# The output product of a gated feed-forward by seven half-size products

## The chip, the cores and the metric

The program runs on one NeuronCore of a Trainium2 chip. TensorE (PE in the profile) multiplies, and its weight loads are listed apart (PEld). VectorE (DVE), ScalarE (ACT) and GpSimd (POOL) work element by element. SyncE (SP) only issues transfers here, and so do ACT and POOL beside their other work. Each engine takes its own instructions in order and waits for the others by semaphores. The metric is the device time of one execution in microseconds; of several executions the median is given.

## What is computed

For each of B = 4 batches, with N = 6016 rows and C = 256 columns, columns of q and k are normalised over the rows, s = knᵀ qn is a 256x256 matrix, a is its softmax, and x = v a. All 24064 rows of x then go through a gated feed-forward with 1536 hidden columns:

```python
s = kn.transpose(0, 2, 1) @ qn / tau          # 256x256 for each batch
a = exp(s - max) / sum
x = (v @ a).reshape(24064, 256)
gate = 1 / (1 + exp(-(x @ w_gate)))           # w_gate, w_val: 256x1536
val = x @ w_val
out = (gate * val) @ w_out                    # w_out: 1536x256
```

## The kernel before, in words

The matrix a is not applied to v. For each batch it is multiplied into the two weight matrices once (`gh_mms`, `gh_store`), which gives G = a w_gate and H = a w_val, so that gate and val come straight from v.

The 6016 rows of a batch are 47 tiles of 128 rows. They are worked through in 12 chunks (`ci` 0 to 11) of 4 tiles, the last of 3: 48 chunks in all. A chunk has 12 steps, here called slots (`f` 0 to 11), one for each 128 hidden columns. A slot does this (`glu`, L414):

- PE forms ps_gate (2 matmuls of 512 columns, one PSUM bank) and ps_val (2 more) from the transposed v;
- ACT writes g_sb, the sigmoid of ps_gate (L435);
- DVE multiplies ps_val by g_sb into hT (L436), which is hidden-by-row, so that it can be the stationary operand of the product that follows;
- PE does 4 matmuls of 256 columns of the output product of the chunk *before* this one (`out_mms`, L442): hT is loaded as weights, w_out is streamed, and 12 of them make one 128-row tile of the output in ps_o.

A finished ps_o is copied to out_sb by DVE in the slot after (`flush`, L458, copy at L462), and when a chunk's last tile is copied, SP stores it. All pools for ps_gate, ps_val and ps_o have two buffers, so the gate matmuls of slot f+2 need the sigmoid of slot f, and the val matmuls of slot f+2 need the product of slot f.

The order is written by hand (`manual_schedule`): what stands first in the program text comes first on each engine. Into the slots of batch b, `side_work` (L548) puts the preparation of batch b+1:

- chunks 0 to 7: loads of q and k (`load_qk`, issued on POOL, converted to bf16 on the way), the matmuls of s (`score`, 94 pairs of 256 columns), and for the norms the squares of q and k and their sums (`acc_square`, L209, and `acc_add`, L218, both on DVE);
- chunk 8: the sums are folded (`acc_fold`, six DVE steps);
- chunks 9 and 10 ("block" chunks): the output matmuls of the chunk before are not interleaved, but stand as one block of 48 after the 12 slots, and beside them run `wide_sqrt`, `wide_inv`, `wide_scale` and `exps`, whose functions need other tables on ACT than the sigmoid;
- chunk 11: G and H of the next batch.

Batch 3 has no side work. v is loaded by POOL two chunks ahead (`load_v`), and SP transposes it by DMA. At the start the whole q and k of batch 0 are loaded with `qkpool` of 8 buffers, then the weights; w_out comes in one POOL transfer in the first slot of the first chunk (`load_w_out`, L151). The end of the last chunk is written apart (`last_rows`, L466).

## Time and profile before

| | |
|---|---|
| median of 3 runs | 829.14 us (828.76 to 829.39) |
| profiled execution, first to last instruction | 827.4 us |
| mean granted TensorE clock | 0.996 |
| PE, DVE, ACT, POOL busy | 97%, 71%, 47%, 10% |
| matmuls of the output product | 2244 of 256 columns and 24 of 128 |
| a slot without side work | 1.30 us |
| a block chunk (198.54 to 214.14) | 15.60 us |

The profiled execution has no time beside its span; the median of the runs is 1.7 us above the span, and that 1.7 us is taken as what lies around it. Each line of the groups gives engine, operation, output and inputs, the shapes, how many, then busy time and mean duration, then the idle time of the engine just before. A line of the timeline begins with start and duration in us, and runs of the same instruction are merged ("x8"); matmuls overlap, so the spacing of a run is its length less one duration, divided by the number less one.

### The profile page before, as it was taken

What the parts mean: (1) busy time and instruction counts of PE and PEld (TensorE: products, weight loads), DVE (VectorE), ACT (ScalarE), POOL (GpSimd) and SP (SyncE); (2) the same over time, 40 slices, a digit from 0 to 9 for tenths busy, and PEclk for the clock granted to TensorE, in tenths of its full rate; (3) what the DMA queues carried; (4) which work ended last, traced back from release to release, by engine and by line L of the source; (5) the groups of instructions that cost most, each with busy time, mean ns of one, the idle gap of its engine ahead of it and who ended that gap; (6) DMA issues with size and microseconds to landing.
All of it is one profiled execution on the core that took longest, in us unless ns stands there. A gap on an engine that the chain in (4) does not pass through costs nothing.

```text
span 827.4 us, 13618 instructions
## 1 busy us (share of the span) xinstructions
PE 806.2 (97%) x5122; PEld 498.6 (60%) x5134; DVE 590.3 (71%) x1023; ACT 392.0 (47%) x643; POOL 79.0 (10%) x151
## 2 busy tenths in 40 slices
PE   3899999999999999999999999999999999999998
PEld 2556666665665666665575666666566566666666
DVE  5777877787667777778757777777766666666665
ACT  3754444446644444445654444444655444444442
POOL 4432100002201100000221010000000000000000
PEclk9899999999999999999999999999999999999999
DMA  9999723327746443223976452223322323322211
GB/s 213 206 201 189 133 52 90 61 52 140 158 85 118 96 90 61 52 52 87 153 141 126 78 110 57 51 64 74 64 62 63 72 52 85 59 58 69 47 36 71
DMA packets 77874, 77.17 MB, mean 93 GB/s; under 512 B 50672, under 2 KB 55792, under 8 KB 77808
## 3 DMA queue, kind: packets, MB, share of 16 engines
q0 software_dynamic: 22768, 38.81, 28.2%
q1 hardware_dynamic: 54752, 36.91, 17.6%
q8 instruction: 40, 0.66, 0.3%
q10 hardware_dynamic: 288, 0.59, 0.2%
q14 instruction: 26, 0.21, 0.1%
HBM read 78.64 MB, written 24.64 MB: 125 GB/s over the span
## 4 chain that ended last, share of the span: by engine, by line
PE 94%; DMA 4%; DVE 1%; issue 0%; ACT 0%; POOL 0%; ACTq 0%; POOLq 0%
PE ps_o L88 30%; PE ps_val L88 29%; PE ps_gate L88 29%; PE ps_s L88 4%; DMA k_sb<-in_k_dram 3%; PE ps_gh L88 2%; DMA w_gate<-in_moe_w_gate_dram 1%; DVE hT L436 0%; ACT g_sb L435 0%; DVE sq L184 0%; PE ps_end L88 0%; PE ps_n L88 0%; DVE gh_G L385 0%; POOL q_sb L98 0%; PE ps_tp L403 0%
## 5 line engine op out<-in xcount | busy, mean ns | idle before, releaser
L436 DVE TENSOR_TENSOR hT<-ps_val,g_sb 128x512 bf16<-128x512 f32 (+1 forms) x576 | 391.2, 680 | 204.6 <-ACT g_sb L435 200.3
L435 ACT ACTIVATE g_sb<-ps_gate 128x512 bf16<-128x512 f32 (+1 forms) x576 | 338.2, 588 | 387.0 <-PE ps_gate L88 380.9
L88 PE MATMUL ps_gate<-vT,gh_G 128*128 128x512 bf16 (+1 forms) x1152 | 337.5, 375 | 0.2
L88 PE MATMUL ps_val<-vT,gh_H 128*128 128x512 bf16 (+1 forms) x1152 | 337.5, 375 | 0.3
L88 PE MATMUL ps_o<-w_out_sb,hT 128*128 128x256 bf16 x2244 | 324.9, 273 | 0.0
L88 PEld LDWEIGHTS <-hT 128*128 128x128 bf16 x2268 | 221.0, 98 | 124.6
L88 PEld LDWEIGHTS <-gh_H 128*128 128x128 bf16 x1152 | 112.7, 98 | 131.4 <-issue 1.0
L88 PEld LDWEIGHTS <-gh_G 128*128 128x128 bf16 x1152 | 112.3, 98 | 37.8 <-DVE gh_G L385 0.4
L462 DVE COPY out_sb<-ps_o 128x256 f32<-128x256 f32 x187 | 77.4, 414 | 12.6 <-PE ps_o L88 12.6
L88 PE MATMUL ps_s<-k_sb,q_sb 128*128 128x256 bf16 x376 | 70.1, 289 | 15.9 <-DMA k_sb<-in_k_dram 8.5
L108 POOL DMA_DIRECT2D v_sb<-in_v_dram x48 | 25.5, 532 | 609.5 <-DMA vT<-v_sb 473.8
L88 PEld LDWEIGHTS <-q_sb 128*128 128x128 bf16 x376 | 38.7, 103 | 24.2 <-issue 9.9
L223 DVE TENSOR_TENSOR acc<-acc,sq 128x1024 bf16<-128x1024 bf16 (+1 forms) x66 | 44.2, 670 | 0.0
L184 DVE TENSOR_TENSOR sq<-q_sb 128x1024 bf16<-128x1024 bf16 (+2 forms) x42 | 28.0, 667 | 1.1 <-DMA q_sb<-in_q_dram 1.1
L98 POOL DMA_DIRECT2D q_sb<-in_q_dram x44 | 24.3, 552 | 28.3 <-PE ps_s L88 10.7
L98 POOL DMA_DIRECT2D k_sb<-in_k_dram x44 | 24.0, 546 | 15.5 <-DMA k_sb<-in_k_dram 10.1
L184 DVE TENSOR_TENSOR sq<-k_sb 128x1024 bf16<-128x1024 bf16 (+2 forms) x34 | 22.4, 658 | 0.1
L182 ACT ACTIVATE sq<-k_sb 128x1024 bf16<-128x1024 bf16 (+1 forms) x11 | 10.7, 1010 | 11.9 <-DMA k_sb<-in_k_dram 11.9
L88 PE MATMUL ps_gh<-w_gate,e_sb 128*128 128x512 bf16 x41 | 12.7, 379 | 1.3 <-DMA w_gate<-in_moe_w_gate_dram 1.2
L88 PE MATMUL ps_gh<-w_val,e_sb 128*128 128x512 bf16 x45 | 13.5, 379 | 0.2
L88 PEld LDWEIGHTS <-e_sb 128*128 128x128 bf16 x112 | 10.2, 97 | 5.7 <-ACT e_sb L324 1.3
L435 ACT ACT_TABLE_LOAD x6 | 7.7, 1283 | 9.0 <-PE ps_gate L88 9.0
(68 smaller groups left out, 122.5 us busy)
## 6 DMA issues: line engine op xcount, KB each, us to landing
out_dram<-out_sb SPq DMA_DIRECT2D x44, 512.0 KB, 2.9
v_sb<-in_v_dram POOLq DMA_DIRECT2D x44, 256.0 KB, 3.9
q_sb<-in_q_dram POOLq DMA_DIRECT2D x35, 256.0 KB, 6.3
k_sb<-in_k_dram POOLq DMA_DIRECT2D x35, 256.0 KB, 7.1
q_sb<-in_q_dram POOLq DMA_DIRECT2D x4, 512.0 KB, 11.5
k_sb<-in_k_dram POOLq DMA_DIRECT2D x4, 512.0 KB, 13.4
out_dram<-out_sb SPq DMA_DIRECT2D x3, 384.0 KB, 3.5
w_gate<-in_moe_w_gate_dram POOLq DMA_DIRECT2D x3, 256.0 KB, 8.1
```

What stands on the lines that cost most here:

```text
L88: nc.tensor.matmul(out, lhsT=lhsT, rhs=rhs, start=start, stop=stop, **kw)
L98: nc.gpsimd.dma_start(out=tl[:, :nt, :], in_=rows(src, b)[:, t0 : t0 + nt, :])
L108: nc.gpsimd.dma_start(out=v_sb[:, :nt, :], in_=rows(v, b)[:, t0 : t0 + nt, :])
L182: nc.scalar.activation(out=sq[:, :nt, :], in_=src[:, :nt, :], func=ACT.Square)
L184: engine.tensor_tensor(out=sq[:, :nt, :], in0=src[:, :nt, :], in1=src[:, :nt, :], op=ALU.mult)
L223: nc.vector.tensor_tensor(out=acc[:, :nt, :], in0=acc[:, :nt, :], in1=st[b]["sq", w][:, :nt, :], op=ALU.add)
L435: nc.scalar.activation(out=g_sb[:, :n], in_=ps_gate[:, :n], func=ACT.Sigmoid)
L436: nc.vector.tensor_tensor(out=hts[b, ci][:, f, :n], in0=ps_val[:, :n], in1=g_sb[:, :n], op=ALU.mult)
L462: nc.vector.tensor_copy(out=out_sb[:, s, :], in_=ps)
```

## The change

The output product is done by Strassen's scheme. For a pair of 128-row tiles (tile p of the first half of the chunk and tile p of its second half), the hidden blocks (even and odd) and the two halves of the output columns, a 2x2 by 2x2 block product is formed with 7 products in place of 8. Each product is 6 matmuls of 128 columns, so a chunk of 4 tiles has 84 of these in place of 48 of 256. The chunks of 3 tiles do one pair so and the third tile as before; the last chunk of all is as before.

- Sums of hT blocks: 10 DVE instructions per chunk of 128x768 (`a_sum`), five (g = 0, hidden blocks 0 to 5) in slots 6 to 10 of the chunk itself, five (g = 1, blocks 6 to 11) in slots 0 to 4 of the next chunk, each behind the product into hT of that slot.
- Sums of w_out blocks: w_out is loaded as three fp32 pieces by SP into a pool of two buffers shared with the first q and k tiles; POOL converts it and forms the five sums (`sum_w_out`).
- Copies from PSUM: for each pair one of 512 and one of 384 columns, on ACT (`evict`), into m_sb.
- Recombination: five POOL instructions per pair (`combine`), then the store (in slot 4 of the chunk after the next).
- The squares of q and k for batches 1 to 3 go from DVE to ACT; g_sb is fp32.
- Buffers: qkpool 8 to 5, sqpool 3 to 2.

The diff, cut to its core:

```diff
+A_SUMS = (
+    ((0, 1), ALU.subtract, (1, 1)),
+    ((0, 0), ALU.add, (1, 1)),
+    ((0, 0), ALU.add, (0, 1)),
+    ((1, 0), ALU.add, (1, 1)),
+    ((1, 0), ALU.subtract, (0, 0)),
+)
+B_SUMS = (
+    ((1, 0), ALU.subtract, (0, 0)),
+    ((0, 1), ALU.subtract, (1, 1)),
+    ((1, 0), ALU.add, (1, 1)),
+    ((0, 0), ALU.add, (1, 1)),
+    ((0, 0), ALU.add, (0, 1)),
+)
+PRODUCTS = (
+    ((1, 1), 0),
+    ((0, 0), 1),
+    (0, 2),
+    (1, 3),
+    (2, (1, 1)),
+    (3, (0, 0)),
+    (4, 4),
+)
+FIRST_BANK = 4
...
-    qkpool = pool("qkpool", 8)
-    sqpool = pool("sqpool", 3)
+    f32pool = pool("f32pool", 2)
+    qkpool = pool("qkpool", 5)
+    sqpool = pool("sqpool", 2)
+    spool = pool("spool", 1)
+    mpool = pool("mpool", 2)
...
-    first_f32 = [consts.tile([P, nt, C], FP32, name=f"first{w}") for w in range(2)]
+    first_f32 = [f32pool.tile([P, TPC, C], FP32, tag="f32", name=f"first{w}") for w in range(2)]
...
-    def load_w_out():
-        nc.gpsimd.dma_start(out=w_out_sb, in_=moe_w_out.rearrange("(t p) c -> p t c", p=P))
+    w_sums = consts.tile([P, len(B_SUMS), FC // 2, P], BF16)
+    w_f32 = {}
+    def load_w_out(n):
+        w_f32[n] = f32pool.tile([P, TPC, C], FP32, tag="f32", name="w_f32")
+        nc.sync.dma_start(
+            out=w_f32[n], in_=moe_w_out.rearrange("(t p) c -> p t c", p=P)[:, n * TPC : (n + 1) * TPC, :]
+        )
+    def sum_w_out(n):
+        w = w_f32.pop(n)
+        nc.gpsimd.tensor_copy(out=w_out_sb[:, n * TPC : (n + 1) * TPC, :], in_=w)
+        for m, ((k0, c0), op, (k1, c1)) in enumerate(B_SUMS):
+            nc.gpsimd.tensor_tensor(
+                out=w_sums[:, m, n * 2 : (n + 1) * 2, :],
+                in0=w[:, k0::2, ds(c0 * P, P)],
+                in1=w[:, k1::2, ds(c1 * P, P)],
+                op=op,
+            )
...
-        if g == 0:
-            nc.vector.tensor_tensor(out=acc, in0=src, in1=src, op=ALU.mult)
-        else:
-            st[b]["sq", w] = squares(b, t0, nt, w, nc.vector)
+        st[b]["sq", w] = squares(b, t0, nt, w, nc.scalar, acc if g == 0 else None)
...
-        g_sb = gpool.tile([P, CH], BF16, tag="g", name="g_sb")
+        g_sb = gpool.tile([P, CH], FP32, tag="g", name="g_sb")
+    sums = {}
+    def a_sum(b, ci, g, m):
+        nt = groups[ci][1]
+        half = nt // 2
+        hT = hts[b, ci]
+        if m == 0:
+            sums[b, ci, g] = spool.tile(
+                [P, len(A_SUMS), FC // 4, CH // 2], BF16, tag=f"s{g}", name="sums", bufs=2 - g
+            )
+        (r0, k0), op, (r1, k1) = A_SUMS[m]
+        f0, f1 = g * (FC // 2), (g + 1) * (FC // 2)
+        nc.vector.tensor_tensor(
+            out=sums[b, ci, g][:, m, :, : half * P],
+            in0=hT[:, f0 + k0 : f1 : 2, ds(r0 * half * P, half * P)],
+            in1=hT[:, f0 + k1 : f1 : 2, ds(r1 * half * P, half * P)],
+            op=op,
+        )
-    def out_mms(b, ci, n0, n1):
-        t0, nt = groups[ci]
+    pending = []
+    stores = []
+    def out_tile(b, ci):
+        if (b, ci) not in ffn:
+            ffn[b, ci] = opool.tile([P, TPC, C], FP32, tag="osb", name="out_sb")
+        return ffn[b, ci]
+    def combine(b, ci, p, m):
+        half = groups[ci][1] // 2
+        blocks = out_tile(b, ci).rearrange("p t (h c) -> p (t h) c", c=P)
+        c00, c11 = 2 * p, 2 * (half + p) + 1
+        ends = blocks[:, c00 : c11 + 1 : c11 - c00, :]
+        t = m[:, 2:7:4, :]
+        nc.gpsimd.tensor_tensor(out=t, in0=t, in1=m[:, 3:4, :].to_broadcast([P, 2, P]), op=ALU.add)
+        nc.gpsimd.tensor_tensor(out=t, in0=t, in1=m[:, 4:6, :], op=ALU.subtract)
+        for n, mids in enumerate((c00 + 1, c11 - 1)):
+            nc.gpsimd.tensor_tensor(
+                out=blocks[:, mids, :], in0=m[:, 1 - n, :], in1=m[:, 4 + n, :], op=ALU.add
+            )
+        nc.gpsimd.tensor_tensor(out=ends, in0=t, in1=m[:, 0:2, :], op=ALU.add)
+    def out_work(b, ci):
+        nt = groups[ci][1]
+        half = nt // 2
-        for n in range(n0, min(n1, nt * FC)):
-            s, f = divmod(n, FC)
-            if n == 0:
-                ffn[b, ci] = opool.tile([P, TPC, C], FP32, tag="osb", name="out_sb")
+        work = []
+        def product(state, p, n, i):
+            a, w = PRODUCTS[n]
+            bank, first = (0, 0) if n < FIRST_BANK else (1, FIRST_BANK)
+            if n == first and i == 0:
+                state[bank] = pso.tile([P, CH], FP32, tag="o", name="ps_o")
+            g, j = divmod(i, FC // 4)
+            if isinstance(a, tuple):
+                lhsT = hT[:, 2 * i + a[1], ds((a[0] * half + p) * P, P)]
+            else:
+                lhsT = sums[b, ci, g][:, a, j, ds(p * P, P)]
+            rhs = w_out_sb[:, 2 * i + w[0], ds(w[1] * P, P)] if isinstance(w, tuple) else w_sums[:, w, i, :]
+            mm(
+                state[bank][:, ds((n - first) * P, P)],
+                lhsT,
+                rhs,
+                start=(n == first and i == 0),
+                stop=(i == FC // 2 - 1),
+                skip_group_check=True,
+            )
+            if i == FC // 2 - 1 and n in (FIRST_BANK - 1, len(PRODUCTS) - 1):
+                pending.append((evict, state, bank, p))
+        def evict(state, bank, p):
+            if bank == 0:
+                state["m"] = mpool.tile([P, len(PRODUCTS), P], FP32, tag="m", name="m_sb")
+            n0, n1 = (0, FIRST_BANK) if bank == 0 else (FIRST_BANK, len(PRODUCTS))
+            m = state["m"]
+            nc.scalar.copy(m[:, n0:n1, :], state[bank][:, : (n1 - n0) * P].rearrange("p (n c) -> p n c", c=P))
+            if bank == 1:
+                combine(b, ci, p, m)
+                if p == half - 1 and nt % 2 == 0:
+                    stores.append((b, ci))
+        def single(state, s, f):
-                ffn["ps"] = pso.tile([P, C], FP32, tag="o", name="ps_o")
-            mm(ffn["ps"], hT[:, f, ds(s * P, P)], w_out_sb[:, f, :], f == 0, f == FC - 1)
+                state["ps"] = pso.tile([P, CH], FP32, tag="o", name="ps_o")
+            mm(state["ps"][:, :C], hT[:, f, ds(s * P, P)], w_out_sb[:, f, :], f == 0, f == FC - 1)
-                pending.append((ffn[b, ci], s, ffn["ps"], b, ci))
-    pending = []
+                pending.append((evict_single, state, s))
+        def evict_single(state, s):
+            nc.scalar.copy(out_tile(b, ci)[:, s, :], state["ps"][:, :C])
+            stores.append((b, ci))
+        for p in range(half):
+            state = {}
+            for n in range(len(PRODUCTS)):
+                for i in range(FC // 2):
+                    work.append((1, product, state, p, n, i))
+        if nt % 2:
+            state = {}
+            for f in range(FC):
+                work.append((2, single, state, nt - 1, f))
+        return work
+    def run_work(work, share):
+        left = sum(w[0] for w in work)
+        upto = left * share
+        done = 0
+        while work and done < upto:
+            cost, fn, *args = work.pop(0)
+            fn(*args)
+            done += cost
-            out_sb, s, ps, b, ci = pending.pop(0)
+            fn, *args = pending.pop(0)
+            fn(*args)
+    def store():
+        while stores:
+            b, ci = stores.pop(0)
-            nc.vector.tensor_copy(out=out_sb[:, s, :], in_=ps)
-            if s == nt - 1:
-                nc.sync.dma_start(out=out_rows[b][:, t0 : t0 + nt, :], in_=out_sb[:, :nt, :])
+            nc.sync.dma_start(out=out_rows[b][:, t0 : t0 + nt, :], in_=ffn.pop((b, ci))[:, :nt, :])
+    def end_rows(b, ci, s):
+        hT = hts[b, ci]
+        ps = pso.tile([P, CH], FP32, tag="o", name="ps_o")
+        for f in range(FC):
+            mm(ps[:, :C], hT[:, f, ds(s * P, P)], w_out_sb[:, f, :], f == 0, f == FC - 1)
+        nc.vector.tensor_copy(out=out_tile(b, ci)[:, s, :], in_=ps[:, :C])
...
-                at(0, load_w_out)
+                for i in range(FC // TPC):
+                    at(i, load_w_out, i)
+                    at(i + 2, sum_w_out, i)
...
-                if prev is not None and not block:
-                    out_mms(*prev, f * TPC, (f + 1) * TPC)
+                if prev is not None:
+                    if f == 4:
+                        store()
+                    if not block:
+                        run_work(work, 1 / (FC - f))
+                    if f < len(A_SUMS):
+                        a_sum(*prev, 1, f)
+                if f >= FC // 2 and f - FC // 2 < len(A_SUMS) and (b, ci) != (B - 1, NCH - 1):
+                    a_sum(b, ci, 0, f - FC // 2)
...
-                    out_mms(*prev, s * FC, (s + 1) * FC)
+                    run_work(work, 1 / (TPC - s))
+            if prev != (B - 1, NCH - 1):
+                work = out_work(*prev)
+    flush()
-        out_mms(*prev, s * FC, (s + 1) * FC)
-        flush()
+        end_rows(*prev, s)
+    store()
```

## The prediction

> **What bounds the kernel now.** I read the page first, engines and then the chain.
>
> ```profile
> PE 806.2 (97%) x5122; PEld 498.6 (60%) x5134; DVE 590.3 (71%) x1023; ACT 392.0 (47%) x643; POOL 79.0 (10%) x151
> PE 94%; DMA 4%; DVE 1%; issue 0%; ACT 0%; POOL 0%; ACTq 0%; POOLq 0%
> ```
>
> PE is the bound from end to end; the 4% of DMA is the load of batch 0. So matmul time saved is time saved, as long as the other engines keep up. Next the groups, shapes kept apart, for the prices:
>
> ```profile
> L436 DVE TENSOR_TENSOR hT<-ps_val,g_sb 128x512 bf16<-128x512 f32 x528 | 364.4, 691 | 180.5 <-ACT g_sb L435 178.8 <-PE ps_gate L88 0.4
> L435 ACT ACTIVATE g_sb<-ps_gate 128x512 bf16<-128x512 f32 x528 | 315.1, 597 | 369.1 <-PE ps_gate L88 369.1
> L223 DVE TENSOR_TENSOR acc<-acc,sq 128x1024 bf16<-128x1024 bf16 x60 | 40.9, 682 | 0.0
> L184 DVE TENSOR_TENSOR sq<-q_sb 128x768 bf16<-128x768 bf16 x3 | 1.6, 550 | 0.0
> L237 DVE TENSOR_TENSOR two<-two 128x256 f32<-128x256 f32 x6 | 2.5, 415 | 0.0
> L182 ACT ACTIVATE sq<-k_sb 128x1024 bf16<-128x1024 bf16 x10 | 10.1, 1049 | 11.6 <-DMA k_sb<-in_k_dram 11.6
> masks.py:199 POOL TENSOR_SCALAR_AFFINE_SELECT ident_f<-ident_f 128x128 f32<-128x128 f32 x1 | 0.3, 292 | 0.1
> ```
>
> Then the timeline: one slot of batch 3, four DVE instructions back to back, the matmul spacings of 256 and 128 columns, and ACT and PE around the two block chunks.
>
> ```profile
> 701.73 0.59 PE L88 MATMUL ps_gate<-vT,gh_G 128*128 128x512 bf16 x2
> 702.36 0.60 ACT L435 ACTIVATE g_sb<-ps_gate 128x512 bf16<-128x512 f32 x1 [0.70 <-PE ps_gate L88]
> 702.59 0.60 PE L88 MATMUL ps_o<-w_out_sb,hT 128*128 128x256 bf16 x4
> 702.99 0.69 DVE L436 TENSOR_TENSOR hT<-ps_val,g_sb 128x512 bf16<-128x512 f32 x1 [0.61 <-ACT g_sb L435]
> ...
> 58.18 0.69 DVE L436 TENSOR_TENSOR hT<-ps_val,g_sb 128x512 bf16<-128x512 f32 x1 [0.83 <-ACT g_sb L435]
> 58.79 0.41 DVE L462 COPY out_sb<-ps_o 128x256 f32<-128x256 f32 x1
> 59.12 0.68 DVE L214 TENSOR_TENSOR acc<-q_sb 128x1024 bf16<-128x1024 bf16 x1
> 59.72 0.69 DVE L436 TENSOR_TENSOR hT<-ps_val,g_sb 128x512 bf16<-128x512 f32 x1
> ...
> 822.69 1.51 PE L88 MATMUL ps_end<-w_out_sb,hT 128*128 128x128 bf16 x24
> 198.54 5.40 PE L88 MATMUL ps_o<-w_out_sb,hT 128*128 128x256 bf16 x48
> ...
> 200.63 1.28 ACT L435 ACT_TABLE_LOAD   x1
> 216.05 0.91 ACT L332 ACTIVATE e_sb<-x_sb,shift 128x256 bf16<-128x256 f32 x2 [0.24 <-DVE x_sb L274]
> ```
>
> From a slot's first gate matmul, the sigmoid starts at 0.63, the output matmuls at 0.86, the product into hT at 1.26 us. DVE instructions overlap: 0.61 from the product to the next, 0.60 from a 0.68 add. Matmul spacing: (5.40-0.27)/47 = 0.109 for 256 columns, (1.51-0.22)/23 = 0.056 for 128, each with new weights.
>
> **A. Matmuls, -23.9 us.** 2220 of 256 columns (242.2 us) become 44 x 84 + 3 x 42 = 3822 of 128 (214.4) and 36 of 256 (3.9). A slot shrinks from 1.30 to 0.86 + 7 x 0.056 = 1.26. The nearest row for narrow matmuls is the burst of 24 at the end; between wide ones they may be slower, bounded by the 256-column spacing of 0.109 (third rival), or no better than 0.056. I take 0.056.
>
> The Trainium skill, "TensorE: Matmul & The Clock Gate", section "Back-to-back issue gap", speaks against the change: for a stream of weight load and matmul pairs it gives about 81 ns at 128 columns. By that A would be 3822 x 0.081 + 3.9 - 242.2 = +71 us; the burst's 0.056 decides here.
>
> **Engines beside PE.** An a_sum is 768 elements from two SBUF inputs: 0.55 by the row of squares, 0.47 to the next instruction. DVE loses 187 copies and, in batches 1 to 3, the squares, and gains 10 sums a chunk: 12 x 0.61 + 10 x 0.47 = 12.0 of 15.1 us. With 3 adds (0.60) it is 13.8 of 17.6 in a side chunk, where score pairs make a slot 1.26 + 0.21 = 1.47. The fp32 gate costs nothing: 256 elements from two fp32 inputs take 415 ns, one element a cycle with the same overhead as the product's 691 for 512. ACT: 12 x 0.60, two copies of 0.60 and two of 0.49, three squares of 1.05, 12.5 of 17.6; a square makes the next sigmoid at most 0.2 late, and ps_gate's buffer is wanted two slots on, 2 x 1.26 - 0.63 - 0.60 = 1.3 after it. Loads stand behind `combine` on POOL for up to some 3 us; they run 12 to 20 slots ahead. The store on SP waits for POOL, and behind it stands only the transposition of the next chunk, ten slots later. The DVE time removed gains nothing: 200 us of the product's idle time was waiting for the sigmoid. The smaller q/k pool is covered by the queue of loads, at worst part of D.
>
> **B. Sums that come late, +10 us (0 to 15).** PE needs sums 2, 3, 4 of the second half in slots 3, 4, 5, and DVE forms them in slots 2, 3, 4, each behind that slot's product. Done at 1.26 + 0.61 + 0.55 = 2.42 after the gate matmul; a hand-over of 0.03 (ACT to DVE above) and a weight load of 0.11 make it 2.56. Matmuls 27, 33 and 39 of the 84 first read them, at 1.26 + 0.86 + 6, 5, 4 x 0.056 = 2.45, 2.40, 2.34. PE waits 0.11, then 0.16 less that, then 0.22 less the second: 0.33 a chunk. Ten chunks of batch 3: 3.3. In side chunks the slot is 0.21 longer and only sum 4 is late, because an add stands in slot 3: 0.2 x 20 = 4. In chunk 8 the folds put 1.5 us on DVE in slots 2 to 4: 0.9 x 3 = 2.7. Matmuls behind a waiting weight load wait too, and with them the next gate. The ends: 0 if the hand-over is 0.2 quicker, 15 if it is 0.1 slower.
>
> **C. Block chunks, +15 us (5 to 20).** Here a slot of PE is 0.86 but DVE needs 1.08. Val matmuls of slot 11 wait for the product of slot 9: 1.26 + 9 x 0.61 + 8 x 0.47 + 0.69 = 11.2 against 9.9 of PE alone, 1.3 in chunk 9. In chunk 10 the first sigmoid is also late: its table load ran inside the block (200.63), but now the last copy from PSUM, after the block, stands before it: 0.2 + 0.49 + 1.28 = 1.97 instead of 0.64 after the block's end; 2.6. And in chunk 10's block the first copy stands behind the exps, which end 2.8 after its start; 3.4 against 2.36 when the bank is wanted, 1.05. Together 4.9, three batches. The low end leaves the 1.3 and a third of the rest, the high end adds a third.
>
> **D. Start, +5 us (0 to 10).** Two of w_out's three fp32 pieces (1.05 MB) go out as soon as the first tiles are converted, into the loads that bound the start (about 210 GB/s in the page's slices): 5 us if they count in full, 2.5 if the read side counts; 3. POOL then has three times a copy and five sums, some 12 us, inside a first chunk of 15 (38.2 to 53.6), with loads behind them, and the third piece waits for the first sums: 2 more.
>
> **E. DVE and POOL, +13 us (0 to 50).** No row shows a POOL tensor_tensor. 256 elements lie between DVE's 0.415 and four times the 0.292 of one input of 128 elements, 1.17; I take 0.6, and 0.35 for 128. Five make a burst of 2.7 us from 1.8 after a chunk's start, over the first three sums. Whether they hinder each other no row shows: the 66 adds at L223, with two inputs, keep 681 to 684 ns beside POOL's DMA issues, which gives the low end 0; losing a whole POOL instruction at each meeting is the high end: 1.8 less DVE's spare 0.35 in plain chunks and 0.8 in side chunks, 10 x 1.4 + 20 x 1.0 + 3 x 1.4 + 6 x 2 = 50. The row is nearest to 0 but shows POOL making descriptors, not reading tiles, so I take a quarter of the span, what half an instruction lost at each meeting gives: 0.5 x 13 + 0.1 x 20 + 6 x 0.8 = 13.
>
> The Trainium skill, "SBUF — State Buffer", section "Who interferes with whom", also speaks against the change: a VectorE instruction with two SBUF inputs and a GpSimd one that reads SBUF share a port, and the later is blocked until the first has ended. By that E is 13 to 50, not 0; nothing here shows it yet.
>
> **Sum.** -23.9 + 10 + 15 + 5 + 13 = +19. On the profiled execution 827.4 + 19 = 846.4 of span, and with the 1.7 around it 848 against the median of 829.1. A difference under 0.2% (1.7 us) could not be told from none.
>
> **Rivals.** (1) Faster, 815: the sums are not late. The place is DVE's chain product-sum in slots 2 to 4; it decides from 0.2 us: if matmul reads the sums that much earlier than I reckon, or DVE starts that much sooner, B is 0, C falls to 5, E, hidden in that slack, to 0: 829 - 24 + 5 + 5. For it: DVE has a fifth of its time free. Against: product and sum stand in a row, and PE's need falls 0.1 to 0.2 before. (2) DVE becomes the bound through POOL, E at 35 to 50: 870 to 885. For it: 2 x 2.7 us of POOL a chunk lie mostly over sums. (3) Narrow matmuls between wide ones need a weight load's 0.107 each (four loads in 0.53 before four matmuls): 3822 x 0.107 - 238 = +171, 1043 with the rest. Against: loads of 98 ns overlap in the burst of 24. (4) A and the rest cancel: 829.
>
> **Chances.** The forecast with E up to 35 (832 to 870) 0.53; (2) 0.14; (3) 0.04; (1) 0.24; (4) 0.05. So faster 0.24, same 0.05, slower 0.71. The range 812 to 876 leaves out 2 in 10: a third of (1), rather more than half of (2), and (3). The likeliest case's own is 832 to 870.
>
> **What will show it.** Right: PE's busy share falls; PE or its weight loads wait for DVE sums in slots 3 to 5; the stretch from one block to the next grows from 10.4 to over 12; ps_o spacing of 0.056 in the blocks. a_sum durations well over 0.55 beside POOL show E. Wrong: no waits for the sums (then about 815), or sums of 0.9 us because their blocks lie apart (then DVE is the bound everywhere).

## The result and the profile after

The changed kernel takes 888.21 us, median of 4 runs (887.03 to 889.01), beside 829.26 us for the kernel before on the same chip: 1.071 times as long, 95% interval 1.0695 to 1.0725. The forecast was 848 with a range to 876, so the direction was right and the size was not: the loss is 59 us where 19 were reckoned. The profiled execution spans 887.2 us, at a granted clock of 0.982 (the share of full speed at which the profile says PE was clocked; 0.996 before).

The page of the changed kernel, engines and the chain by engine:

```profile
PE 812.7 (92%) x6772; PEld 501.3 (57%) x6772; DVE 739.6 (83%) x1236; ACT 533.0 (60%) x900; POOL 422.1 (48%) x623
PE 71%; DVE 12%; DMA 6%; ACT 5%; issue 5%; POOL 1%; DVEq 0%; ACTq 0%; POOLq 0%
```

The chain went through PE for 94% of the span before, and now only for 71%; DVE, ACT, DMA and issue (time in which an engine waited for nothing that the profile shows) hold 28%. The groups, shapes kept apart, that answer to the priced rows (output, input, count, busy us, mean ns, then idle time before):

```profile
L482 DVE TENSOR_TENSOR hT<-ps_val,g_sb 128x512 bf16<-128x512 f32 x528 | 360.5, 684 | 91.2 <-ACT g_sb L481 54.3 <-PE ps_val L119 29.9
L481 ACT ACTIVATE g_sb<-ps_gate 128x512 f32<-128x512 f32 x528 | 315.2, 598 | 283.8 <-PE ps_gate L119 276.7 <-DVE acc L269 3.5 <-DVE hT L482 2.7
L499 DVE TENSOR_TENSOR sums<-hT 128x768 bf16<-128x768 bf16 x440 | 288.8, 656 | 0.0
L269 DVE TENSOR_TENSOR acc<-acc,sq 128x1024 bf16<-128x1024 bf16 x60 | 46.2, 770 | 0.0
L283 DVE TENSOR_TENSOR two<-two 128x256 f32<-128x256 f32 x6 | 4.1, 677 | 0.0
L522 POOL TENSOR_TENSOR m_sb<-m_sb 128x256 f32<-128x256 f32 x91 | 65.8, 723 | 422.4 <-ACT m_sb L564 422.4
L525 POOL TENSOR_TENSOR out_sb<-m_sb 128x128 f32<-128x128 f32 x182 | 112.6, 638 | 0.0
```

The fp32 gate costs nothing, as said (598 and 684 ns, against 597 and 691). What reads PSUM keeps its length; each DVE instruction that reads two SBUF inputs has grown: the sums take 656 ns instead of the 550 forecast, the adds 770 instead of 682, the fold of 256 elements 677 instead of 415. The waits of the changed kernel (total us, times, longest):

```profile
PE ps_s L119 <- DMA k_sb<-in_k_dram: 34.3, 7, 12.5
PEld L119 <- DVE sums L499: 21.3, 42, 1.0
PE ps_o L119 <- DVE sums L499: 13.0, 30, 0.9
```

The waits for sums were foreseen. The first line was not: PE waits up to 12.5 us for a transfer of k in mid-kernel. And a slot of batch 3 from the timeline:

```profile
743.66 0.73 POOL L522 TENSOR_TENSOR m_sb<-m_sb 128x256 f32<-128x256 f32 x1 [3.58 <-ACT m_sb L564]
743.86 0.95 DVE L499 TENSOR_TENSOR sums<-hT 128x768 bf16<-128x768 bf16 x1
...
745.33 0.54 DVE L499 TENSOR_TENSOR sums<-hT 128x768 bf16<-128x768 bf16 x1
...
745.36 0.55 PE L119 MATMUL ps_o<-w_sums,sums 128*128 128x128 bf16 x7
```

Seven narrow matmuls between wide ones are (0.55 - 0.22)/6 = 0.055 us apart, so the price of A was right. The sum that starts 0.2 us after a POOL instruction takes 0.95 us, the one in the next slot, which starts just ahead of POOL's next instruction (745.33 against 745.35), 0.54.

Taking the start of each chunk's first gate matmul from the two traces shows where the time is. Chunk (b, ci) is chunk ci of batch b; differences to the kernel before in us, those of the later experiments beside them ("sums first" is described below, as are the others):

| | after | loads ahead | sums first | sums first, POOL reads nothing | second assembly |
|---|---|---|---|---|---|
| until the first gate | +3.3 | +3.4 | +3.3 | +3.3 | -0.3 |
| chunk (0,0) | +1.3 | +1.4 | +1.5 | +1.6 | +0.9 |
| chunks (1,0) and (2,0) | +29.2 | -0.6 | -0.6 | -0.6 | -0.6 |
| chunk 8, three batches | +6.5 | +6.5 | +6.1 | +0.7 | -1.4 |
| chunk 9, three batches | +3.1 | +3.1 | +3.3 | +1.9 | +1.8 |
| chunk 10, three batches | +11.2 | +11.2 | +11.5 | +9.6 | +0.6 |
| chunk 11, three batches | +2.8 | +2.8 | -0.5 | -1.1 | +4.8 |
| (0,1) and the other 20 chunks with side work | +3.1 | +3.2 | -11.7 | -11.9 | -11.0 |
| chunks 0 to 10 of batch 3 | -2.8 | -2.8 | -5.8 | -5.8 | -5.8 |
| last chunk | +2.0 | +2.0 | +1.1 | -0.6 | +1.1 |
| span | +59.8 | +30.1 | +8.4 | -2.8 | -9.7 |

Half the loss lies in two chunks. In the timeline of the kernel before, POOL's queue two and a half chunks ahead of chunk (1,0), which starts at 237.70:

```profile
194.92 0.53 POOL L108 DMA_DIRECT2D v_sb<-in_v_dram  x1 [15.15 <-DMA vT<-v_sb]
195.44 0.54 POOL L98 DMA_DIRECT2D q_sb<-in_q_dram  x1
195.96 0.55 POOL L98 DMA_DIRECT2D k_sb<-in_k_dram  x1
```

and after the change, where POOL and PE stand inside chunk (1,0) itself:

```profile
254.42 0.72 POOL L522 TENSOR_TENSOR m_sb<-m_sb 128x256 f32<-128x256 f32 x1 [6.06 <-ACT m_sb L564]
...
257.39 0.57 POOL L139 DMA_DIRECT2D v_sb<-in_v_dram  x1
257.95 0.54 POOL L129 DMA_DIRECT2D q_sb<-in_q_dram  x1
258.48 0.55 POOL L129 DMA_DIRECT2D k_sb<-in_k_dram  x1
...
266.58 0.58 PE L119 MATMUL ps_s<-k_sb,q_sb 128*128 128x256 bf16 x2 [12.48 <-DMA k_sb<-in_k_dram]
```

The code puts these loads at slot max(0, s0 - 20). For the first three groups of batches 2 and 3, s0 - 20 is negative, so all three go out in slot 0: in program order the first, which is used in that same slot, has no lead at all, and the next two have 8 and 16 slots instead of 20. The lead of 42 us was made by POOL itself, which had only loads in its queue and ran ahead of the program until the buffers were full. Now the recombination of chunk (0,10)'s second pair stands in front of them, and waits for a copy from PSUM that ACT makes in slot 0 of chunk (1,0).

### The profile page after: what moved, and what is told of

Same layout as the page of the kernel before. It is cut to its first block, busy times and chain, and to the rows that moved or that the text cites. A ratio compares the mean times of both kernels' runs of the same rounds, so it can differ in the third digit from the quotient of the medians.

```text
span 887.2 us, 17830 instructions
## 1 busy us (share of the span) xinstructions
PE 812.7 (92%) x6772; PEld 501.3 (57%) x6772; DVE 739.6 (83%) x1236; ACT 533.0 (60%) x900; POOL 422.1 (48%) x623
## 4 chain that ended last, share of the span: by engine, by line
PE 71%; DVE 12%; DMA 6%; ACT 5%; issue 5%; POOL 1%; DVEq 0%; ACTq 0%; POOLq 0%
PE ps_gate L119 23%; PE ps_o L119 22%; PE ps_val L119 21%; DVE sums L499 6%; DVE hT L482 5%; DMA k_sb<-in_k_dram 5%; PE ps_s L119 3%; ACT g_sb L481 2%; PE ps_gh L119 2%; ACT sq L231 2%; DMA w_gate<-in_moe_w_gate_dram 1%; ACT m_sb L564 0%; ACT L304 0%; DVE acc L269 0%; DVE two L279 0%
## 5 line engine op out<-in xcount | busy, mean ns | idle before, releaser
L481 ACT ACTIVATE g_sb<-ps_gate 128x512 f32<-128x512 f32 (+1 forms) x576 | 338.3, 589 | 294.9 <-PE ps_gate L119 287.1
L499 DVE TENSOR_TENSOR sums<-hT 128x768 bf16<-128x768 bf16 (+1 forms) x470 | 303.3, 645 | 0.0
L522 POOL TENSOR_TENSOR m_sb<-m_sb 128x256 f32<-128x256 f32 x91 | 65.8, 723 | 422.4 <-ACT m_sb L564 422.4
L119 PEld LDWEIGHTS <-sums 128*128 128x128 bf16 x2730 | 184.7, 98 | 98.7 <-DVE sums L499 21.3
L119 PE MATMUL ps_o<-w_sums,sums 128*128 128x128 bf16 x1638 | 152.5, 220 | 1.2 <-DVE sums L499 0.9
L119 PE MATMUL ps_o<-w_out_sb,sums 128*128 128x128 bf16 x1092 | 108.1, 219 | 12.2 <-DVE sums L499 12.2
L525 POOL TENSOR_TENSOR out_sb<-m_sb 128x128 f32<-128x128 f32 x182 | 112.6, 638 | 0.0
L119 PEld LDWEIGHTS <-hT 128*128 128x128 bf16 x1176 | 82.9, 98 | 47.4 <-issue 6.2
L564 ACT COPY m_sb<-ps_o 128x512 f32<-128x512 f32 (+1 forms) x182 | 95.6, 527 | 9.7 <-PE ps_o L119 9.6
L119 PE MATMUL ps_o<-w_sums,hT 128*128 128x128 bf16 x1092 | 90.1, 220 | 4.7 <-ACT m_sb L564 4.2
L523 POOL TENSOR_TENSOR m_sb<-m_sb 128x256 f32<-128x256 f32 x91 | 80.2, 881 | 7.1
## 6 DMA issues: line engine op xcount, KB each, us to landing
k_sb<-in_k_dram POOLq DMA_DIRECT2D x4, 512.0 KB, 14.8
```

The source lines that it names most:

```text
L119: nc.tensor.matmul(out, lhsT=lhsT, rhs=rhs, start=start, stop=stop, **kw)
L481: nc.scalar.activation(out=g_sb[:, :n], in_=ps_gate[:, :n], func=ACT.Sigmoid)
L499: nc.vector.tensor_tensor(out=sums[b, ci, g][:, m, :, : half * P], in0=hT[:, f0 + k0 : f1 : 2, ds(r0 * half * P, half * P)], in1=hT[:, f0 ...
L522: nc.gpsimd.tensor_tensor(out=t, in0=t, in1=m[:, 3:4, :].to_broadcast([P, 2, P]), op=ALU.add)
L523: nc.gpsimd.tensor_tensor(out=t, in0=t, in1=m[:, 4:6, :], op=ALU.subtract)
L525: nc.gpsimd.tensor_tensor(out=blocks[:, mids, :], in0=m[:, 1 - n, :], in1=m[:, 4 + n, :], op=ALU.add)
```

## Experiments

Theory Q: the loss in chunks (1,0) and (2,0) is the lost run-ahead of POOL's queue. Rival: it is the q and k pool cut from 8 buffers to 5. For the rest: late sums (B), first sigmoids and exps late behind PSUM copies on ACT (C), the early w_out loads (D), and DVE lengthened beside POOL's reads (E).

### The first loads ahead, and two changes to the kernel before

Three kernels: the changed one with its first loads moved (`e1_loads_ahead`); the kernel before with a tiny POOL instruction in the way (`e2_before_mark`); and the kernel before with 5 buffers (`e6_before_five`).

```diff
 e1: side_work(b)
+        for g, (t0, nt) in enumerate(groups):
+            if n + 1 < B and g * 8 < 20:
+                at(NCH * FC + g * 8 - 20, load_qk, n + 1, t0, nt)
...
-            at(max(0, s0 - (12 if b == 0 else 20)), load_qk, n, t0, nt)
+            if b == 0 or s0 >= 20:
+                at(s0 - (12 if b == 0 else 20), load_qk, n, t0, nt)
 e2: flush, behind the copy of a chunk's last tile
+                mark = sqpool.tile([P, 1], FP32, tag="mark", name="mark")
+                nc.gpsimd.tensor_copy(out=mark, in_=out_sb[:, s, :1])
 e6:
-    qkpool = pool("qkpool", 8)
+    qkpool = pool("qkpool", 5)
```

> The changed kernel with one thing moved: the loads of the first three groups of q and k of batches 2 and 3 are issued 20 slots ahead, in chunks 10 and 11 of the batch before, instead of in slot 0 of the batch that uses them. Queue theory (the loads stood on POOL behind the recombination, which waits for the end of the chunk before, so they went out only in slot 0, 8.7 us before they were wanted): the two stretches of 30 us for the first chunk of batches 1 and 2 fall to about 16, and the time from 888 to 859 (855 to 863). Buffer theory (the loads were late because qkpool has 5 buffers in place of 8): no buffer is added, so at most a few us, 880 to 888. Contention theory (DVE and POOL hinder each other all along and this is the main loss): 885 to 888.

> The kernel before with one tiny POOL instruction (a copy of one column) put behind the last copy from PSUM of each chunk, in front of the loads of the next; everything else as before, 8 buffers, no recombination. Queue theory: POOL can no more run ahead with the loads, which go out in slot 0 of batches 1 and 2, and the time rises by 25 to 30 us, to 854 to 859. Buffer theory and contention theory: 829 to 831.

> The kernel before with qkpool of 5 buffers in place of 8, nothing else. Queue theory: POOL still runs ahead, five groups deep, 829 to 832. Buffer theory: the loads of the first groups are late, 845 to 859.

Measured: loads ahead 859.0 us (ratio 1.0359, 1.0343 to 1.0374), the mark 852.77 (1.0283, 1.0262 to 1.0304), five buffers 829.2 (0.9997, 0.9987 to 1.0008). In the first, chunks (1,0) and (2,0) fall to 15.32 us each and nothing else moves by more than 0.1. In the second only these two chunks grow, by 11.7 and 12.0 us. POOL's queue with the mark, from the timeline:

```profile
239.93 0.18 POOL L465 COPY mark<-out_sb 128x1 f32<-128x1 f32 x1 [18.91 <-DVE out_sb L462]
240.44 0.53 POOL L108 DMA_DIRECT2D v_sb<-in_v_dram  x1 [0.33 <-issue]
240.96 0.54 POOL L98 DMA_DIRECT2D q_sb<-in_q_dram  x1
241.48 0.55 POOL L98 DMA_DIRECT2D k_sb<-in_k_dram  x1
```

0.18 us of POOL work, once a chunk, costs 23.5 us: the wait in the queue does it, not the work. PE's wait in chunk (1,0) is

```profile
248.74 0.58 PE L88 MATMUL ps_s<-k_sb,q_sb 128*128 128x256 bf16 x2 [9.76 <-DMA k_sb<-in_k_dram]
```

The run came out a little under its expected range. The mark waits for the copy alone and not for five instructions behind it, so k's load goes out 4.0 us after the chunk's first gate and not 5.7, and PE waits 9.8 us and not 12.5. The rival of the buffers falls. The lost run-ahead is worth 887.2 - 857.5 = 29.7 us of span (29.2 by the medians, as the profiled execution was the slowest of its four).

### The sums ahead of the product

`e4_sums_first` is the kernel with loads ahead, with each sum in front of the product into hT of its slot, rather than behind it.

```diff
+                if prev is not None and f < len(A_SUMS):
+                    a_sum(*prev, 1, f)
+                if f >= FC // 2 and f - FC // 2 < len(A_SUMS) and (b, ci) != (B - 1, NCH - 1):
+                    a_sum(b, ci, 0, f - FC // 2)
                 glu(b, ci, f, (lambda: gh(0, 4, pso, "o", act=False)) if first else None)
 ...
-                    if f < len(A_SUMS):
-                        a_sum(*prev, 1, f)
-                if f >= FC // 2 and f - FC // 2 < len(A_SUMS) and (b, ci) != (B - 1, NCH - 1):
-                    a_sum(b, ci, 0, f - FC // 2)
```

> The kernel with the loads ahead, and each sum of hT blocks put in front of the product into hT of its slot instead of behind it. Late-sum theory (PE waits 0.2 to 0.5 us a chunk, more in chunks 8, because product and sum stand in a row on DVE): the waits for sums go from PE and its weight loads (34 us in the changed kernel) and the time falls by 8 to 25 us against the kernel with the loads ahead, to 834 to 851. DVE-bound theory (DVE is the bound wherever PE waits, so that the order of its work is indifferent): within 3 us of the kernel with the loads ahead, with the wait moved to the products into hT.

Measured: 837.62 us (ratio 1.01, 1.0083 to 1.0116), 21.4 us less. The weight loads' wait for sums, 21.3 us before, is

```profile
PEld L119 <- DVE sums L499: 1.3, 7, 0.3
```

and chunks 3 to 7 of the batches with side work and chunks 1 to 10 of batch 3 now gain 0.48 to 0.55 us each over the kernel before, the whole of A. The sums still take 661 ns in the mean: beside POOL they are as long as they were, but in these chunks nobody waits for them.

### POOL reads nothing

In `e3_pool_no_reads` (loads ahead, sums late) and `e11_sums_first_no_reads` (sums first) the five recombination instructions are five fills that read no tile; the recombination is left out.

```diff
-        nc.gpsimd.tensor_tensor(out=t, in0=t, in1=m[:, 3:4, :].to_broadcast([P, 2, P]), op=ALU.add)
 ... (the other four too)
+        for n in range(2):
+            nc.gpsimd.memset(ends, 0.0)
+        for mids in (c00 + 1, c11 - 1):
+            nc.gpsimd.memset(blocks[:, mids, :], 0.0)
+        nc.gpsimd.memset(ends, 0.0)
```

> The changed kernel with the early loads (859.0 us), and GpSimd's five recombination instructions of each row pair replaced by five fills with zero that read nothing; the recombination is left out. What is asked is how much of the time is the lengthening of VectorE's instructions beside GpSimd's reads (step E). Contention theory: with GpSimd reading nothing the 768-element sums fall from a mean of 660 ns to about 550, the accumulation adds from 770 to about 680, and the time falls by the 13 us that the prediction put on it, to 846 (843 to 851). Late-sum theory: the sums are late by their place behind the hT product, and a shorter sum beside it helps little in the chunks with side work; only the chunks where VectorE itself is full (8, 9 and 10 of each batch) gain, some 1 us each, so 850 to 856. If fills disturb VectorE as reads do: 859, and durations as before.

> The version with sums first (837.6 us) with the recombination on GpSimd replaced by five fills that read nothing (the recombination is left out, as in the run that did this with the sums late: 859.0 to 839.7 us, 19.3 us). Theory that the lengthened VectorE instructions cost time only where VectorE is full or the sums are last in its queue: with the sums first only chunks 8 (1.7 us), 9 (0.5 us) and 10 (0.2 us) of three batches and the last chunk (1 us) gain, so 829.5 (827 to 832). Theory that the lengthening costs time everywhere: 19 us again, 818.

Measured: 839.66 us with the sums late (ratio 1.0125, 1.011 to 1.0141), 19.3 us less; 826.11 with the sums first (0.9964, 0.995 to 0.9978), 11.5 us less. DVE's groups in the first of the two:

```profile
L499 DVE TENSOR_TENSOR sums<-hT 128x768 bf16<-128x768 bf16 x440 | 242.1, 550 | 0.0
L269 DVE TENSOR_TENSOR acc<-acc,sq 128x1024 bf16<-128x1024 bf16 x60 | 41.0, 684 | 0.0
```

The sums are back at the forecast's 550 ns and the adds at 684: POOL's reads, not its presence, lengthen them: the 77 sums that overlap a fill take 548 to 552 ns, while in the changed kernel the 229 that overlap one of POOL's reading instructions take 759 in the mean, and the other 211 take 539 to 550. (The Trainium skill, "SBUF — State Buffer", section "Who interferes with whom", says just this: a DVE instruction with two SBUF inputs contends with a GpSimd one that reads SBUF, not with one that only writes. These runs agree.) Both results lie outside what was expected of them, below: 839.7 is under the 843 at which the prediction's 13 us ended, and 826.1 under 827. So the lengthening costs 20 us of span with the sums late and 11 with them first. Where it sits with the sums first, the table shows: 5.4 us in chunk 8, where DVE is full, 1.4, 1.9 and 0.6 in chunks 9 to 11, 1.7 in the last chunk, and 0.2 in all the rest. The fills are also shorter than what they replace (POOL's busy time is 197 us with the sums late, against 422), so part of the 1.7 at the end may be POOL's own time; that part was not split. The fills no longer wait for ACT's copies either, but that gave nothing elsewhere: after 70 us, in the two kernels that recombine, neither PE, DVE nor ACT waits for a load, and for POOL only DVE does, once, for 1.0 us or less at the very end.

### The block chunks

Chunk 10 still takes 3.8 us more with the sums first. Its start, from the timeline of that kernel, gates from 410.44:

```profile
411.14 1.28 ACT L481 ACT_TABLE_LOAD   x1
412.43 1.09 ACT L481 ACTIVATE g_sb<-ps_gate 128x512 f32<-128x512 f32 x2
413.06 0.69 DVE L482 TENSOR_TENSOR hT<-ps_val,g_sb 128x512 bf16<-128x512 f32 x1 [1.86 <-ACT g_sb L481]
413.08 0.59 PE L119 MATMUL ps_gate<-vT,gh_G 128*128 128x512 bf16 x2 [0.75 <-ACT g_sb L481]
```

The first sigmoid starts 1.99 us after the first gate matmul, where step C said 1.97. Two causes may hold: ACT's copies, or DVE, which has 12 x 0.68 + 10 x 0.55 = 13.7 us of durations to do (12.0 by the prediction's spacings, since they overlap) in a stage of 10.3. `e7_block_sums` takes five sums out of the slots, `e8_block_copies` gives the copies of these blocks back to DVE; both start from sums first.

```diff
 e7
-                if f >= FC // 2 and f - FC // 2 < len(A_SUMS) ...
+                if not block and f >= FC // 2 and f - FC // 2 < len(A_SUMS) ...
 ... (in the block)
                     run_work(work, 1 / (TPC - s))
                     flush()
+                    for m in ((0, 1), (2,), (3,), (4,))[s]:
+                        a_sum(b, ci, 0, m)
 e8
-            nc.scalar.copy(m[:, n0:n1, :], ...)
+            copy = nc.vector.tensor_copy if b + 1 < B and ci in (8, 9) else nc.scalar.copy
+            copy(m[:, n0:n1, :], ...)
```

> The version with sums first (837.6 us), with the five sums of the first half of a chunk's own hT, in chunks 9 and 10 of batches 0 to 2, moved out of the gate slots into the block of output products behind them. Theory that VectorE is full in these gate stages (12 hT products of 0.68 us and 10 sums of 0.55 us, 13.7 us, against 10.3 us of TensorE): chunk 9 falls by some 0.5 us and chunk 10 by some 1.4 us, three times each, so 832 (829 to 835). Theory that the late first sigmoid alone (PSUM copies and a table load on ScalarE, step C) makes these chunks long: within 1 us of 837.6.

> The version with sums first (837.6 us), with the four PSUM copies of each block of output products (executed in chunks 9 and 10 of batches 0 to 2) on VectorE again, as they were before the change, and all others on ScalarE. Theory of step C (copies on ScalarE keep the first sigmoid and the exps waiting): the first sigmoid of chunks 10 and 11 comes 1.0 us earlier, and the 0.9 us wait of TensorE for a copy behind the exps goes; 1.5 to 2.5 us a batch, so 832 (829 to 834). Theory that VectorE is the bound of these chunks: the four copies (2.1 us) come on top of it, and nothing is won or up to 2 us a chunk lost, so 837 to 850.

Measured: 833.52 us for the sums (ratio 1.0052, 1.0037 to 1.0067), 4.1 less; 833.34 for the copies (1.0049, 1.0034 to 1.0064), 4.3 less. Each theory named a part: chunk 10 falls by 1.2 us with the sums moved and by 1.5 with the copies moved. With the sums moved the first sigmoid still starts at 1.99, and the gate stage is 0.9 us shorter. With the copies moved it starts at 0.63 again, but the copies now stand on DVE, the first product follows the sigmoid only after 1.25 us (0.03 before), and the stage is 0.7 us shorter; the other 0.8 lie in the block. So both causes hold.

### w_out later

`e9_w_out_late` issues w_out's three fp32 loads from ACT in slots 0 to 2, with the POOL sums in slots 4 to 6 and batch 1's first loads somewhat earlier.

```diff
-        nc.sync.dma_start(
+        nc.scalar.dma_start(
             out=w_f32[n], ...
-                    at(i + 2, sum_w_out, i)
+                    at(i + 4, sum_w_out, i)
+                    at(7, cast_w_out, i)
...
+                at(max(0, s0 - (18 if b == 0 else 20)), load_qk, n, t0, nt)
```

> The version with sums first (837.6 us), with the three fp32 loads of w_out issued by ScalarE in slots 0 to 2 of the first chunk instead of at 6.4 us by SyncE; sums of w_out in slots 4 to 6, its casts behind them, q and k of batch 1 loaded 18 slots ahead instead of 12. Theory of step D (the early loads share the DMA engines with the first batch's q and k): the first gate starts at 38.2 us again instead of 41.6, and the time falls by 3.3 us to 834.3 (833.5 to 836), less what chunk (0,1) loses where the sums of w_out come later than its first products (up to 3 us). Theory that the start is late by GpSimd's own casts and sums: the first gate stays at 41.6 us, and the time at 837.6 or above.

Measured: 839.55 us (ratio 1.0123, 1.0106 to 1.014), 1.9 more. The first gate does start at 38.00 again, 3.6 us earlier, so those loads did hold up the start. But chunk (0,1) loses 6.4 us, because the loads now take 10.8 to 13.3 us to land and the sums of w_out come late:

```profile
59.20 0.48 PE L119 MATMUL ps_o<-w_sums,hT 128*128 128x128 bf16 x3 [3.28 <-POOL w_sums L196]
59.47 1.06 PE L119 MATMUL ps_gate<-vT,gh_G 128*128 128x512 bf16 x2
```

The second line shows why a 3.28 us wait cost 6: the matmuls behind it run at half speed (two in 1.06 us instead of 0.59) for another 5 us, at a granted clock of 0.50 from 59.2 to 64.3.

### All edits together

`e10_all` puts together: loads ahead, sums first, block sums and block copies as above, the other five sums of chunks 9 and 10 in every second slot, w_out's loads on POOL behind the other weights, and no folds (PE sums the accumulators of the norms itself):

```diff
-        for i in range(6):
-            at(8 * FC + 2 + i, acc_fold, n, *divmod(i, 3))
...
-        fold_q, fold_k = s["fold"]
-        norm_mms(ps, (fold_q,), 2, True, True, (0,))
-        for u in range(2):
+        fold_q, fold_k = s["acc"]
+        norm_mms(ps, (fold_q,), TPC, True, True, (0,))
+        for u in range(TPC):
```

> All that the runs so far point to, put together: the version with sums first (837.6 us), first-half sums of chunks 9 and 10 in the block (alone: -4.1 us), block copies on VectorE (alone: -4.3 us), the other five sums of these chunks in every second slot; TensorE adds up the bf16 accumulators of the norms itself (2 wide and 4 narrow matmuls a batch, some 0.6 us) in place of VectorE's folds (4 us a batch, in chunk 8, where VectorE is full); the fp32 loads of w_out in GpSimd's queue behind the other weights, ahead of q and k of batch 1. By the terms: block sums and copies together -7 to -9, the spreading -2 to -4, no folds -3 to -6, first gate 3.3 us earlier less up to 3 us at chunk (0,1): 820 us, range 814 to 827. Theory that Strassen's saving on TensorE is real but VectorE takes it all back elsewhere: 829 or above.

Measured: 826.67 us, ratio 0.9976 (0.9967 to 0.9985): faster than both, but 6.7 us short of the sum of its terms. The folds and the start gave their part (chunk 8 of three batches from +6.1 to -1.4 against the kernel before, first gate at 38.18). Chunk 10 did not (+9.1 in all, where either edit alone had left +7.9 and +6.9), because DVE now went into it with work left over:

```profile
403.49 0.60 ACT L483 ACTIVATE g_sb<-ps_gate 128x512 f32<-128x512 f32 x1 [2.29 <-PE ps_gate L119]
...
406.39 0.68 DVE L484 TENSOR_TENSOR hT<-ps_val,g_sb 128x512 bf16<-128x512 f32 x1
...
407.13 0.59 PE L119 MATMUL ps_val<-vT,gh_H 128*128 128x512 bf16 x2 [1.95 <-DVE hT L484]
```

The chunk's first product into hT comes at 406.39, though its sigmoid had ended at 404.09: a reciprocal, two PSUM copies and a sum stood in front of it. Two edits that each paid alone had filled the same 5 us of DVE. `e12_second` spreads them:

```diff
-            copy = nc.vector.tensor_copy if b + 1 < B and ci in (8, 9) else nc.scalar.copy
+            copy = nc.vector.tensor_copy if b + 1 < B and ci in (8, 9) and p == 1 else nc.scalar.copy
...
-            (9, 3, wide_inv, n, 1),
+            (10, 0, nc.scalar.preload_act_table, ACT.Exp),
+            (10, 0, wide_inv, n, 1),
...
-            (10, 0, exps, n, 0),
-            (10, 0, exps, n, 1),
+            (10, 2, exps, n, 0),
+            (10, 2, exps, n, 1),
...
-                    for m in ((0, 1), (2,), (3,), (4,))[s]:
+                    for m in (((0, 1), (2,), (3,), (4,)) if ci == 9 else ((), (0, 1), (2, 3), (4,)))[s]:
...
-        nc.gpsimd.tensor_copy(out=w_out_sb[...], in_=w_f32.pop(n))
+        nc.scalar.copy(w_out_sb[...], w_f32.pop(n))
```

> The assembled version (826.7 us) with VectorE's load in the two blocks of output products set right: in its trace chunk 10 still took 3.0 us more than before the change, because VectorE went into that chunk with copies, a reciprocal and sums still queued (its first hT product came 1.8 us after the sigmoid, one slot of 2.98 us), and chunk (0,1) 2.8 us more, because the casts of w_out stood behind fifteen sums on GpSimd. Now the copies of the first row pair are on ScalarE, the second reciprocal and the exps stand in the next block, two sums of chunk 10 come later, and ScalarE casts w_out. If VectorE's queue at the end of the block is the cause, chunk 10 falls by some 2 to 2.5 us three times and chunk (0,1) by some 2.5 us: 817.5 (814 to 821). If it is the late sigmoid table, nothing moves at chunk 10, and the time is 824 or above.

Measured: 819.97 us, ratio 0.9889 (0.9872 to 0.9905), 9.3 us less than the kernel before and 68 less than the change as it was made. Chunk 10 falls by 2.9 us three times and chunk (0,1) by 2.4; chunk 11 gives 1.7 back each time, as its first product now comes 1.7 us after the sigmoid. What each of these moves gave was not split. The removal of the folds was not tried on the kernel before; its chunk 8 takes 15.60 us, as long as a chunk of batch 3 without side work, so there is no sign that the folds cost it anything.

## Why the prediction was too low

By its own terms, from differences of spans (us):

| step | forecast | measured | from |
|---|---|---|---|
| A, matmuls | -23.9 | -22.4 | the rest of the version with sums first and no POOL reads (-2.8), once C and D are taken out |
| B, late sums | +10 | +13.1 | sums late less sums first, POOL reading nothing: 837.7 - 824.6 |
| C, block chunks | +15 | +14.7 | chunks 9 and 10 of that version, +1.9 and +9.6, and the six gains of 0.53 that they miss |
| D, start | +5 | +4.9 | first gate +3.3, chunk (0,0) +1.6 |
| E, DVE and POOL | +13 | +19.8 | loads ahead, less the same without POOL's reads: 857.5 - 837.7 |
| loads of q and k | 0 | +29.7 | after less loads ahead: 887.2 - 857.5 |
| sum | +19 | +59.8 | |

A is what is left over, so the column adds up by construction; what shows A by itself is the 0.48 to 0.55 us a chunk of the version with sums first. All terms but the loads come to +30.1 where 19 were reckoned, and with the loads ahead the time, 859.0 us, lies inside the range: the loads alone took it out.

- **The step that failed** is the sentence "Loads stand behind `combine` on POOL for up to some 3 us; they run 12 to 20 slots ahead." It costed a shared queue at nothing and named 12 to 20 slots of lead as its cover. For three groups of batches 2 and 3 the slot is max(0, s0 - 20) = 0: the first has no lead in the program, the others 8 and 16 slots, and the one in the trace was run-ahead, which ends with the first instruction on POOL that waits for a late engine. The delay named (3 us behind five instructions) was right: the loads do follow the recombination by 3 us. What was missed is where that puts them: POOL used to be there 42.8 us before chunk (1,0) began, and now the recombination starts 1.7 us after (254.42 against 252.74) and the first load of q 5.2 us after.
- **A** held, and with it the choice of the burst's 0.056 over the higher price; rival (3) is out with 0.055 us between narrow matmuls.
- **B** held in its mechanism and, at the upper end of its range, in its total: PE did wait for the sums; put first in the slot, they left 1.3 us of the weight loads' wait. Its places did not hold, and that the total agrees is partly luck. Of the 13.1 us, batch 3 has 2.0 (3.3 reckoned), the chunks with side work 7.4 (4), chunk 8 nothing (2.7), and chunks 10 and 11 have 4.1 that it did not name.
- **C** held by its amount and by its instructions: the first sigmoid 1.99 us after the first gate, and a second cause, DVE's own length, which it had at 1.3 us a batch.
- **D** held: most of it is the loads at the start, as the run with w_out later shows.
- **E** had the mechanism right and was too small, and the mis-sized part is DVE's spare time. The loss at a meeting was about as taken: with the loads ahead, the 152 sums over 600 ns are 0.32 us longer than the rest in the mean, where half a POOL instruction of 0.6 us was reckoned. But not all of this reached PE (the sums grew by 440 x 0.106 = 47 us), and where it did was not foreseen. The chunks with side work, taken at 0.1 each for a spare of 0.8, lost 0.36, chunk 8 lost 2.0 each time, and the chunks of batch 3, taken at 0.5, lost less than 0.1. The span lost is 19.8 us, well inside 0 to 50. The row that the forecast leaned on is of 60 adds, not 66; the other six have a shorter tile. Rival (2), E at 35 or more, is out, although the time fell just beyond the range it gave.
- Rival (1), sums not late, is out: it ends where the prediction put it only when the program puts the sums first.

B and E overlap: with the sums first, E is 11 us and not 20, and B, measured with POOL reading, is 857.5 - 835.8 = 21.7 and not 13.1. Together they are 32.9 where 23 were reckoned. What each is worth depends on the order in which they are removed; the table takes E off first.

## What to carry to other kernels

An engine that only issues transfers runs ahead of the program, and the lead seen in the trace can be larger than the lead that the code asks for. Before compute is put on such a queue, read for each of its transfers the slot at which the program issues it, not the time at which the trace shows it. On a shared in-order engine, put the instruction that another engine will wait for first in its slot; here that alone was worth 21 us, and it also made a lengthening of 20% harmless in most chunks.

## What the runs showed of the hardware

- After two idle stretches of these runs the clock granted to PE was half, and it stayed so for some 5 us of work. In the changed kernel, windows around the wait in chunk (1,0) (start and end, length, busy us and count of each engine, granted clock, DMA share, GB/s):

```profile
254.00:266.50 12.50, 0.11 (x2) 0.00 (x0) 1.35 (x2) 0.34 (x1) 7.71 (x14) 0.66 0.65 124
266.50:271.60 5.10, 5.02 (x22) 2.69 (x23) 1.23 (x3) 2.14 (x3) 0.00 (x0) 0.50 1.14 207
271.60:276.00 4.40, 4.40 (x39) 2.80 (x37) 2.86 (x7) 2.58 (x5) 0.00 (x0) 1.00 0.66 123
```

  The 12.5 us of waiting and half of 5.1 us make 15.0, less the chunk's gain of 0.28: the 14.8 us that chunk (1,0) lost. A wait of 3.28 us was enough for the same in the run with w_out later. The Trainium skill, "TensorE: Matmul & The Clock Gate", Part 1, has half rate after an idle window of about 3.4 us and full rate after as long a busy one; here 3.28 us of waiting were enough, and the recovery took 5.
- A POOL instruction on two fp32 inputs takes 0.72 us for 256 elements at its shortest; the forecast's 0.6 was 20% low, and where it overlaps one of DVE's sums it took 0.92 (L523 at 744.47, beside the sum at 743.86). L523 takes 723 to 732 ns in the 14 places where none of DVE's two-input instructions overlaps it, and 909 in the mean in the 77 others: the lengthening goes both ways.
- Not only DVE instructions with two SBUF inputs grew. The cast of the folds (L286, one fp32 input of 256 elements) takes 282 ns in the kernel before; in the changed one three of the six, beside POOL's recombination, take 814 to 816 and the other three 278 to 280, and with POOL's reads gone all six take 286 to 290.
